# Six opening products in place of eleven, and weight blocks queued ahead of a table, in a Fourier attention kernel

## The chip, the core and the metric

The kernel runs on one core of a Trainium2 chip. The core has five engines, each with an instruction stream of its own that it works off in order: TensorE (PE in the profile, its weight loads are shown apart as PEld), VectorE (DVE), ScalarE (ACT), GpSimd (POOL) and SyncE (SP), which here issues all transfers. TensorE reads from the core's SBUF memory and writes to PSUM, from which DVE and ACT fetch the results. The metric is the device time of one execution in microseconds (us), the median of three runs.

## What is computed

The reference is a chain of three blocks over 4 batches of 1088 tokens with 128 features. In short:

```python
q_p, k_p = phi(q), phi(k)                      # outer product of two 8-wide projections: 64 features
kv, z = einsum('bhsf,bhsd->bhfd', k_p, v), sum(k_p)
attn  = (q_p @ kv) / (q_p @ z + 1e-6)          # linear attention, 4 heads of 32
x     = attn, heads side by side               # 4 x 1088 x 128
u     = x + real(fft over tokens and features of x)
x2    = u + relu(norm(u) @ w_ch1) @ w_ch2      # channel block
h     = relu(x2 @ w_in); uu, v = halves of h
out   = (uu * (w_spatial @ norm(v) + b)) @ w_out
```

The Fourier transform is computed as matrix products with tables of cosines and sines. [...]

## The kernel before

For each batch the kernel runs these stages. `keys` and `queries` build the features: for each of three chunks of tokens, TensorE projects (`abp`), ACT copies (`ab`), and DVE forms the outer products (`pp`); TensorE then sums keys against values (`kv`, copied to `kvz`), transposes the queries' features (`qps`, copied to `qp` by ACT), and multiplies the two (`nm`); DVE divides (`rd`, `ub`). `fourier_seq` folds the tokens with a product (`rp`) and additions on DVE (`eo`, `fe`, `l_`, `lrb`) and transforms along tokens with the table `tr` (and its rest `trr`) in 16 pairs of passes named `dft`; `fourier_feat` transforms along features with the table `dd` (`ups`, `urm`) and adds to `ub`. `channel` normalises (`un`), transposes (`t`), and runs the channel block (`h_`, `c`) and the first half of the last block (`v_ps`, `v`), ending in `vh` and `vlo`. `spatial` is the large product over tokens (`ac`), three passes for each piece, against the split weights `wsh` and `wsl`, which are made on the way from the loaded `wst`.

`from_f64` turns a block of raw 64-bit weights (`wraw`, 128 x 256 numbers) into 32-bit ones with five DVE instructions (lines 312, 315 to 318), three on ACT (311, 313, 314) and one on POOL (320); `weight` then splits the result into two parts (ACT line 333, POOL line 114). Ten such blocks exist; the buffers of `from_f64` are two deep.

`warm(n)` issues n products of a tile of zeros (`wp<-a`, line 519) that nothing uses. They stand in the program before everything else, after `rp` (10) and ahead of the channel block of batch 0 (20).

The program text writes batch 0's attention and transform, then its channel block, then `keys(1)` and `queries(1)`; a scheduler that weighs priorities and estimated times decides the order on each engine. Products marked with `tc.keep_in_program_order` keep their order among TensorE's. So an edit of the text can move many instructions. The transfers go through SP's queue in the order of the schedule, at most eight outstanding, since a transfer reuses the semaphore of the one eight places before it, and waits for that one's landing. `kt` and `qt` share ten buffers (`kq`), so a transfer for batch 2 also waits until TensorE has read the one whose buffer it takes.

Of the kernel before, what the change touches and what calls it, by code (L numbers as in the profile page):

```python
# [65 lines left out]
def fourier_attention_gmlp_kernel(  # L66
# [258 lines left out]
    def weight_load(tag, *blocks):  # L325
        t = const.tile([P, len(blocks), 512], I32, tag=tag, name="wraw")
        for i, (n, src, k) in enumerate(blocks):
            nc.sync.dma_start(out=t[:, i, :], in_=src.bitcast(I32)[:, 512 * k:512 * k + 512])
            wraw[n, k] = t[:, i, :]
# [8 lines left out]
    def loads(b):  # L338
        for tag, src in (("kt", kT), ("qt", qT)):
            for c in range(3):  # L340
                x = loaded[b, tag, c] = ca.tile([P, 384], F32, tag="kq", bufs=10, name=tag)
                nc.sync.dma_start(out=x, in_=src[b, :, 384 * c:384 * c + 384])
            if b == 0 and tag == "kt":
                nc.sync.dma_start(out=prm, in_=perm)
        for c in range(3):
            vx = loaded[b, "vx", c] = ca.tile([P, 3, 4, 33], F32, tag="vx", bufs=5, name="vx")
            nc.sync.dma_start(out=vx, in_=vt[b, :, 3 * c:3 * c + 3, :, :])
# [168 lines left out]
    def warm(n):  # L516
        wp = psy.tile([P, 512], F32, tag="us", bufs=1, name="wp")
        for i in range(n):
            tc.keep_in_program_order(mm(out=wp, lhsT=wz[:, 0:128], rhs=wz, start=True, stop=True))

    warm(11)
    raw0 = pre.tile([P, 128], I32, tag="un", bufs=2, name="raw")
    nc.sync.dma_start(out=raw0, in_=sblk.bitcast(I32))
    from_f64(raw0, 64, sb_s, True)
# [5 lines left out]
    blocks = [("w1", 0), ("w1", 1), ("w2", 0), ("w2", 1), ("wi", 2), ("wi", 3), ("wi", 0), ("wi", 1), ("wo", 0), ("wo", 1)]  # L530
    srcs = {"w1": w1, "w2": w2, "wi": win, "wo": wout}
    def load_raw(tag, part):
        weight_load(tag, *[(n, srcs[n], k) for n, k in part])

    loads(0)
    nc.sync.dma_start(out=tr, in_=trig)
    nc.sync.dma_start(out=trr, in_=trig_r)
    load_raw("wsl0", blocks[:6])
    nc.sync.dma_start(out=dd, in_=ddft)
    loads(1)  # L540
    load_raw("wsh0", blocks[6:])
# [209 lines left out]
```

## Time and profile before

| | |
|---|---|
| median of 3 runs | 462.87 us (462.74 to 463.55) |
| the profiled execution | 462.66 us, of which the span of the trace is 460.7 us |
| PE busy in the span | 441.3 us (96%) |
| DVE, ACT, POOL busy | 276.4, 191.7 and 68.4 us |
| mean granted clock of TensorE | 0.984 of full |

A busy share is the share of the span in which an engine works at an instruction. For TensorE it includes products that run at the lower of its two clocks (1.2 GHz in place of 2.4 GHz), and the products of zeros. Time is to be had where TensorE stands still, where it runs at the lower clock, or where it computes what nobody uses.

### The profile page before, as it was taken

The page shows a single profiled execution, that of the slowest core. Times are in us where ns is not written, and L with a number is a line of the kernel's source. Part 1 is how long each engine was busy: PE and PEld are TensorE (multiplying, and loading weights), DVE is VectorE, ACT ScalarE, POOL GpSimd, SP SyncE. Part 2 cuts the span into 40 slices and gives each one's busy share as a digit, 9 for nine tenths or more (in the row PEclk, how much of TensorE's full clock was granted, in tenths as well). Part 3 has the DMA queues.
Part 4 walks back from the last instruction along what each step waited for, and adds up shares of the span by engine and source line. Part 5 has one row for each costly group of instructions (what it writes and reads, how often), then busy time and mean ns, then how long its engine had stood idle before and what let it go on. Part 6 is the DMA issues. An engine that isn't in the chain of part 4 may idle for free.

```text
span 460.7 us, 7484 instructions
## 1 busy us (share of the span) xinstructions
PE 441.3 (96%) x2893; PEld 405.5 (88%) x2893; DVE 276.4 (60%) x685; ACT 191.7 (42%) x448; POOL 68.4 (15%) x105
## 2 busy tenths in 40 slices
PE   8889699899999999999999999999999999999996
PEld 7766589567879789899999999999999999999995
DVE  5688988987563596789736363883645456222221
ACT  3545596365223154456524243552423335212221
POOL 2154485572110150000000000000000000000000
PEclk9979799999999999999999999999999999999999
DMA  8992132011003100000000000000000000000000
GB/s 254 359 314 97 52 92 83 0 39 34 0 1 93 38 17 1 0 1 20 14 1 0 18 0 1 18 1 14 2 0 18 0 19 1 14 1 17 1 17 16
DMA packets 13007, 19.29 MB, mean 42 GB/s; under 512 B 1446, under 2 KB 11436, under 8 KB 12844
## 3 DMA queue, kind: packets, MB, share of 16 engines
q1 hardware_dynamic: 12972, 18.82, 12.7%
q8 instruction: 23, 0.38, 0.4%
q14 instruction: 12, 0.10, 0.1%
HBM read 16.58 MB, written 2.23 MB: 41 GB/s over the span
## 4 chain that ended last, share of the span: by engine, by line
PE 77%; issue 9%; DVE 9%; ACT 3%; POOL 1%; POOLq 0%; DVEq 0%; ACTq 0%
PE ac L605 12%; PE ac L604 12%; PE ac L606 12%; PE dft L462 3%; PE v_ps L254 2%; PE v_ps L256 2%; PE c L225 2%; PE c L227 2%; PE c L226 2%; PE v_ps L255 2%; PE nm L408 2%; PE ac L612 2%; PE ac L611 1%; PE u_ps L597 1%; PE u_ps L598 1%
## 5 line engine op out<-in xcount | busy, mean ns | idle before, releaser
L606 PE MATMUL ac<-wsh,vlo 128*128 128x384 f32 (+1 forms) x384 | 126.3, 329 | 2.2 <-POOL vlo L114 2.2
L604 PE MATMUL ac<-wsh,vh 128*128 128x384 f32 (+1 forms) x384 | 126.7, 330 | 0.1
L605 PE MATMUL ac<-wsl,vh 128*128 128x384 f32 (+1 forms) x384 | 126.4, 329 | 0.0
L606 PEld LDWEIGHTS ac<-wsh,vlo 128*128 128x128 f32 x384 | 72.0, 188 | 3.3 <-POOL vlo L114 3.1
L605 PEld LDWEIGHTS ac<-wsl,vh 128*128 128x128 f32 x384 | 72.1, 188 | 1.6 <-issue 0.8
L604 PEld LDWEIGHTS ac<-wsh,vh 128*128 128x128 f32 x384 | 72.1, 188 | 1.5 <-ACT vh L270 0.4
L615 DVE TENSOR_TENSOR uh<-ac,uh 128x384 f32<-128x384 f32 (+1 forms) x48 | 25.4, 529 | 57.0 <-PE ac L612 55.2
L601 ACT ACTIVATE uh<-u_ps 128x384 f32<-128x384 f32 (+1 forms) x48 | 22.6, 471 | 48.0 <-PE u_ps L599 45.5
L114 DVE TENSOR_TENSOR gl<-uh,gh 128x384 fp32r<-128x384 f32 (+1 forms) x48 | 26.2, 548 | 12.9 <-ACT gh L616 12.7
L245 POOL CAST xh<-xh 128x64 fp32r<-128x64 f32 x4 | 2.1, 514 | 201.8 <-ACT xh L242 201.8
L359 DVE TENSOR_TENSOR pp<-ab 128x768 f32<-128x768 f32 x23 | 23.7, 1062 | 11.8 <-ACT ab L355 11.4
L261 DVE BATCH_NORM_STATS2 bst<-vn 128x6 f32<-128x512 f32 x27 | 18.6, 693 | 16.7 <-ACT vn L259 16.6
L616 ACT CAST gh<-uh 128x384 fp32r<-128x384 f32 (+1 forms) x48 | 23.5, 492 | 12.2 <-DVE uh L615 11.9
L259 ACT ACTIVATE vn<-v_ps 128x512 f32<-128x512 f32 x27 | 16.0, 598 | 19.1 <-PE v_ps L256 18.6
L241 DVE TENSOR_TENSOR xt<-c,xt 128x384 f32<-128x384 f32 (+1 forms) x12 | 6.4, 534 | 27.7 <-PE c L227 27.7
L408 PE MATMUL nm<-kvz,qp 128*128 128x66 f32 x144 | 17.4, 271 | 0.0
L408 PEld LDWEIGHTS nm<-kvz,qp 128*128 128x128 f32 x144 | 17.2, 192 | 0.1
L282 ACT CAST vh<-vn 128x1024 fp32r<-128x1024 f32 x12 | 12.6, 1047 | 10.3 <-PE ac L605 8.2
L242 ACT CAST xh<-xt 128x384 fp32r<-128x384 f32 (+1 forms) x12 | 6.0, 497 | 26.0 <-DVE xt L241 26.0
L225 PE MATMUL c<-hh,w 128*128 128x384 f32 (+1 forms) x48 | 16.6, 346 | 0.0
L597 PE MATMUL u_ps<-sxh,wi 128*128 128x384 f32 (+1 forms) x48 | 16.3, 339 | 0.3 <-ACT uh L601 0.3
L227 PE MATMUL c<-hl,w 128*128 128x384 f32 (+1 forms) x48 | 16.3, 340 | 0.0
(714 smaller groups left out, 961.6 us busy)
## 6 DMA issues: line engine op xcount, KB each, us to landing
wst<-in_wsp SPq DMA_DIRECT2D x18, 192.0 KB, 2.8
vx<-in_vt SPq DMA_DIRECT2D x12, 198.0 KB, 4.3
kt<-in_kT SPq DMA_DIRECT2D x12, 192.0 KB, 6.2
qt<-in_qT SPq DMA_DIRECT2D x12, 192.0 KB, 4.4
w2st<-in_wsp SPq DMA_DIRECT2D x9, 160.0 KB, 4.1
tr<-in_trig SPq DMA_DIRECT2D x1, 1096.0 KB
wraw<-in_w SPq DMA_DIRECT2D x4, 256.0 KB, 7.7
wraw<-in_win SPq DMA_DIRECT2D x4, 256.0 KB, 5.2
```

The lines of the kernel that those rows point to most:

```text
L114: eng.tensor_tensor(out=lo, in0=x, in1=hi.bitcast(F32), op=ALU.subtract)
L225: mm(out=c2[:, 0:n], lhsT=wpart("w2", 0, 128 * m, 128), rhs=hh[:, 0:n], start=(m == 0), stop=False)
L227: mm(out=c2[:, 0:n], lhsT=wpart("w2", 0, 128 * m, 128), rhs=hl[:, 0:n], start=False, stop=(m == 3))
L359: (G if [b, tag[0], c] in [[3, 'k', 2]] else V).tensor_tensor(out=pp, in0=a_.unsqueeze(3).to_broadcast([P, 12, 8, 8]), in1=b_.unsqueeze(2) ...
L408: mm(out=nm[:, t, 2 * pr:2 * pr + 2, :].rearrange("p h d -> p (h d)"), lhsT=qp[:, pr, 128 * t:128 * t + 128], rhs=z[:, pr, :], start=True, ...
L597: mm(out=h_[:, 0:n], lhsT=wpart("wi", 0, 128 * m, 128), rhs=xh[:, 0:n], start=True, stop=False)
L601: A.activation(out=uh[:, 0:n], in_=h_[:, 0:n], func=ACTF.Relu)
L604: mm(out=ac[:, 0:n], lhsT=vh[:, k, ms], rhs=wsh[c][:, k, :], start=(k == 0), stop=False)
L605: mm(out=ac[:, 0:n], lhsT=vh[:, k, ms], rhs=wsl[c][:, k, :], start=False, stop=False)
L606: mm(out=ac[:, 0:n], lhsT=vl[:, k, ms], rhs=wsh[c][:, k, :], start=False, stop=False)
L615: V.tensor_tensor(out=uh[:, 0:n], in0=ac[:, 0:n], in1=uh[:, 0:n], op=ALU.mult)
L616: A.copy(out=gh[:, 0:n], in_=uh[:, 0:n])
```

## The change

Two lines differ. The opening products of zeros become six in place of eleven, and the transfers of six blocks of raw weights (`load_raw("wsl0", blocks[:6])`, each 256 KB: both blocks of `w1`, both of `w2`, two of `wi`) are written ahead of the transfers of the transform's table (`tr`, 1096 KB, and `trr`, 137 KB) in place of behind them.

```diff
-    warm(11)
+    warm(6)
     raw0 = pre.tile([P, 128], I32, tag="un", bufs=2, name="raw")
...
     loads(0)
+    load_raw("wsl0", blocks[:6])
     nc.sync.dma_start(out=tr, in_=trig)
     nc.sync.dma_start(out=trr, in_=trig_r)
-    load_raw("wsl0", blocks[:6])
     nc.sync.dma_start(out=dd, in_=ddft)
```

The scheduler answers with another order on every engine. On TensorE, from the ten products after `rp` of batch 0 (names as above; `abp<-sb_s,kt` and the first `kv` here belong to batch 1), the difference reads:

```order
 L519 MATMUL wp<-a_73 128x512 x10
-L353 MATMUL abp<-sb_s,kt 128x2x32 x9
-L353 MATMUL abp<-sb_s,qt 128x2x32 x3
-L376 MATMUL kv<-vx,pp 64x33 x36
-L397 MATMUL qps<-prm,pp 128x128
-L462 MATMUL dft<-tr,l__380 64x274
-L397 MATMUL qps<-prm,pp 128x128 x4
-L462 MATMUL dft<-tr,l__380 64x274 x3
...
+L462 MATMUL dft<-tr,l__375 64x274
+L353 MATMUL abp<-sb_s,kt 128x2x32 x2
+L462 MATMUL dft<-tr,l__375 64x274 x3
```

Batch 1's projections and key sums, which stood between the ten products and the transform, now stand behind it, but for two projections.

On DVE, in the order of before, this stands between the additions of batch 0 (`eo`, `lrb`) and the operands of the transform (`l_`):

```order
L438 TENSOR_TENSOR eo<-ub 128x512
L451 TENSOR_TENSOR lrb<-rs__378 32x63 x2
L312 TENSOR_SCALAR dy<-wraw 128x256
L315 TENSOR_SCALAR dx<-wraw 128x256
L312 TENSOR_SCALAR dy<-wraw 128x256
L315 TENSOR_SCALAR dx<-wraw 128x256
L359 TENSOR_TENSOR pp<-ab 128x768 x4
L447 TENSOR_TENSOR l__380<-fe 128x2x64 x2
```

In the changed kernel the same place on DVE reads:

```order
L316 TENSOR_SCALAR ds<-wraw 128x256
L438 TENSOR_TENSOR eo<-ub 128x512
L451 TENSOR_TENSOR lrb<-rs__373 32x63
L442 TENSOR_TENSOR fe<-eo 128x4x63
L451 TENSOR_TENSOR lrb<-rs__373 32x63
L447 TENSOR_TENSOR l__375<-fe 128x2x64 x2
L438 TENSOR_TENSOR eo<-ub 128x512
```

The four outer products of batch 1 are gone from here to behind the channel block's first instructions, and the first weight blocks' conversions have moved ahead: eight of their DVE instructions now stand between batch 0's sixth `pp` and its first `rd`. On ACT three of them now stand among the six copies of the queries' transposes:

```order
L385 COPY kvz_84<-kv 64x2x33
L311 ACTIVATE dr<-wraw 128x256
L402 COPY qp<-qps 128x384 x2
L313 ACTIVATE dy<-dy,cst 128x256
L402 COPY qp<-qps 128x384 x2
L314 ACTIVATE dy<-dy,cst 128x256
L402 COPY qp<-qps 128x384 x2
```

Before, the six copies followed `kvz` without a break, and the conversions came behind them.

## Rows read from the trace of the kernel before

**Rows 1.** The page, part 2: TensorE's granted clock, in tenths, in 40 slices of the span.

```profile
PEclk9979799999999999999999999999999999999999
```

**Rows 2.** By stage: us; busy PE, PEld, DVE, ACT, POOL; granted clock, DMA share, GB/s.

```profile
0.00:4.00 4.00, 2.43 (x6) 1.95 (x7) 1.86 (x11) 2.41 (x5) 3.14 (x13) 1.00 0.42 120
...
5.80:12.40 6.60, 6.60 (x110) 6.43 (x109) 4.75 (x6) 1.92 (x6) 0.00 (x0) 1.00 1.01 350
...
50.15:57.00 6.85, 6.11 (x20) 5.05 (x21) 6.07 (x17) 3.37 (x9) 2.63 (x4) 0.50 0.02 8
57.00:79.20 22.20, 21.95 (x141) 19.59 (x140) 19.17 (x44) 18.90 (x45) 16.61 (x15) 1.00 0.33 91
79.20:106.50 27.30, 24.00 (x162) 18.03 (x160) 25.55 (x50) 14.05 (x32) 17.48 (x22) 1.00 0.08 22
106.50:460.70 354.20, 347.84 (x2217) 329.18 (x2213) 188.56 (x467) 130.41 (x299) 13.09 (x29) 1.00 0.04 12
```

**Rows 3.** Timeline, 0 to 14 us: start, us, engine, line, operation, out<-in [idle before].

```profile
1.57 4.74 PE L519 MATMUL wp<-a 128*128 128x512 f32 x11 [1.57 <-DVE a L514]
...
3.90 0.22 DVE L320 TENSOR_TENSOR sb_s<-dr,ds 128x64 f32<-128x64 f32 x1
...
6.15 2.12 PE L353 MATMUL abp<-sb_s,kt 128*128 128x64 f32 x18
...
7.45 2.20 SPq L328 DMA_DIRECT2D wraw<-in_w  x4
...
10.21 2.29 PE L376 MATMUL kv<-vx,pp 128*64 128x33 f32 x72
...
11.21 1.83 DVE L359 TENSOR_TENSOR pp<-ab 128x768 f32<-128x768 f32 x2 [0.34 <-PE kv L376]
```

**Rows 4.** Timeline, 12 to 21 us: the queries of batch 0.

```profile
12.43 0.87 PE L397 MATMUL qps<-prm,pp 128*128 128x128 f32 x6
...
14.17 2.10 ACT L402 COPY qp<-qps 128x384 f32<-128x384 f32 x4 [0.25 <-PE qps L397]
...
15.59 3.46 PE L408 MATMUL nm<-kvz,qp 128*128 128x66 f32 x30
...
20.62 0.46 PE L429 MATMUL rp<-ub,prm 128*128 128x128 f32 x2 [1.56 <-DVE ub L418]
```

**Rows 5.** Timeline, 20 to 51 us: from the ten products to the channel block.

```profile
20.83 2.56 PE L519 MATMUL wp<-a 128*128 128x512 f32 x10
...
27.05 3.56 DVE L359 TENSOR_TENSOR pp<-ab 128x768 f32<-128x768 f32 x4
...
28.06 3.23 PE L376 MATMUL kv<-vx,pp 128*64 128x33 f32 x72 [2.05 <-DVE pp L359]
...
31.63 1.18 PE L462 MATMUL dft<-tr,l__380 128*64 128x274 f32 x2
...
38.41 0.62 PE L462 MATMUL dft<-trr,lrb 128*64 128x274 f32 x2
...
41.60 4.84 PE L519 MATMUL wp<-a 128*128 128x512 f32 x20
...
50.15 0.42 PE L199 MATMUL t<-prm,un 128*128 128x128 f32 x1 [3.31 <-DVE un L195]
```

**Rows 6.** Timeline: one step of the transform (a pair of passes) and the next.

```profile
37.02 0.39 PE L462 MATMUL dft<-tr,lz 128*64 128x274 f32 x1
...
37.25 0.39 PE L462 MATMUL dft<-tr,lz 128*64 128x274 f32 x1
```

**Rows 7.** Groups by line and shape, 0 to 60 us: count, busy us, mean ns, idle before.

```profile
L313 ACT ACTIVATE dy<-dy,cst 128x256 int32<-128x256 int32 x10 | 4.9, 504 | 4.3 <-DVE dy L312 4.3
...
L315 DVE TENSOR_SCALAR dx<-wraw 128x256 int32<-128x256 int32 x10 | 2.8, 276 | 0.0
```

**Rows 8.** Spatial weights: first use (timeline), and issue to landing (page, part 6).

```profile
58.41 0.92 ACT L134 CAST wsh<-wst 128x384 fp32r<-128x384 f32 x2
...
wst<-in_wsp SPq DMA_DIRECT2D x18, 192.0 KB, 2.8
```

## The prediction

> **What bounds the kernel now.** I read the profile from the whole to the place. The stages first [rows 2]: from 106.5 us to the end TensorE is busy for 347.8 of 354.2 us, so whatever the change does must reach the end through the time at which this saturated part begins. From 57 to 106.5 us two engines are near full: TensorE 45.95 of 49.5 us, DVE 44.7 of 49.5 us. The opening of 57 us is another thing. There TensorE waits and twice runs at the lower clock [rows 1]; from 50.15 to 57 us the granted clock is 0.50 [rows 2].
>
> The timeline shows who makes it wait. Eleven products of zeros take 0.43 us each (4.74/11), where ten of the same form take 0.256 us later [rows 3, 5]: 0.43 us for 512 columns is the 1.2 GHz level, although the view of stages prints 1.00 there. They are TensorE's first work, and the projections behind them begin at 6.15 us. Then the chain runs through DVE: `rp` waits 1.56 us for `ub` [rows 4], `kv` of batch 1 waits 2.05 us for `pp`, and the transform, from 31.63 to 39.03 us, begins only after DVE's four `pp` of batch 1 (3.56 us) and TensorE's `kv` of batch 1 (3.23 us), which stand ahead of it in the order though it needs neither [rows 5]. The channel block's first transpose comes at 50.15 us after a wait of 3.31 us for DVE [rows 5].
>
> **The change, step by step.** I follow the chain to that first transpose, and then subtract the work that is only put off.
>
> *Five products fewer.* Six end at 1.57 + 6 x 0.43 = 4.15 us. The projections need `sb_s`, ready at 4.12 us [rows 3], and the first `kt`: in the first 4 us 120 GB/s bring 480 KB [rows 2], which covers the 64 KB ahead of it and two chunks of 192 KB. So they begin at about 4.2 in place of 6.15 us. But the six chunks then wait for transfers: the first `qt` has landed by 7.45 us, where SP goes on to `wraw` behind it [rows 3], and at 350 GB/s [rows 2] the other two follow by 0.55 us each, 8.55 us. A chunk of six passes takes 0.7 us (2.12/18 x 6, [rows 3]), so the projections end at 9.3 us, the first sums of `kv` follow at once in place of at 10.21 us, and DVE's last two `pp`, which wait for `kv`, end at 12.1 in place of 13.04 us. Gain 0.9 us of the 2.15 us taken away.
>
> *Raw weights first.* The transfers ahead of both candidates come to 2.0 MB; the six blocks are 1.54 MB, the table 1.23 MB. At 350 GB/s from 7.45 us on, with some 1.0 MB still to land there, the first two blocks land by about 11.7 and the table by 18 us, where it would have landed by 14. The transform cannot ask for it before 24 us (below), so this delay costs nothing; without that cover it would cost the 4 us itself.
>
> *Conversions moved forward.* DVE waited 13.04 to 16.41 us; eight conversion instructions now stand there, 2.2 us at 0.276 us [rows 7], so they fit. On ACT three of them stand among the six `qp` copies: 1.5 us at 0.504 us [rows 7]. The copies ended at 16.27 us [rows 4]; now they end at 16.27 - 0.9 + 1.5 - 0.25 (ACT's own wait there) = 16.6 us. `rp` came 4.35 us behind them, through `nm` and `ub`, and I add 0.4 us for two more conversion instructions between `rd` and `ub` on DVE. So `rp` comes at 21.4 in place of 20.62 us: the gain of the opening is given back, and 0.8 us more.
>
> *The transform moved forward.* From the end of `rp` (21.08 us) to the transform's start (31.63 us) went 10.55 us, 3.56 of them for four `pp` [rows 5] and about 2.7 for ten conversion instructions at 0.276 us [rows 7]. Left are 4.3 us for the operands. I add 0.5 us for POOL's small copies, which now stand behind two conversions of its own. From 21.85 us this gives 26.6 us for the second pass of the transform (the first comes earlier). At full clock a step takes 0.23 us [rows 6], 16 steps 3.7 us, so it ends at 30.3 in place of 39.03 us. From its end to the first transpose went 50.15 - 39.03 = 11.1 us; the chain in it (`ups`, `ub`, statistics on DVE with eleven conversion instructions in place of twelve) is the same, and the twenty products beside it are hidden under DVE. First transpose: 41.4 us, **8.7 us earlier**.
>
> *What is put off.* DVE still has to do four `pp`, 3.56 us, and three conversion instructions, 0.9 us: 4.5 us that were done before 50.15 us. TensorE has three projections (six passes, 0.7 us), 36 products of `kv` (72 passes, 2.3 us by [rows 3]) and six transposes (0.9 us by [rows 4]): 3.9 us. They fall into the stage in which both are over 90% busy [rows 2], so I count them in full: the net gain is 8.7 - 4.5 = 4.2 us by DVE and 4.8 by TensorE. I take the smaller. The five products do not enter again, for the chain has passed them already.
>
> *The queue.* SP's transfers of the spatial weights now stand behind a `qt` of batch 2, whose buffer is free when TensorE has done batch 1's third projection, behind the twenty products: about 38 us (26.6 + 3.7 + 2.6 for `ups` and `urm` + 4.84 [rows 5]). They land 2.8 us after issue; eight of them by about 44 us. ACT's first use came 8.3 us after the first transpose [rows 5, 8], so at 49.7 us now: 5 us of cover, nothing to pay. If the twenty products ran at 0.43 us, 3.8 us of it would go, still nothing.
>
> *The clock.* In the channel block's first 6.85 us the clock was low, after TensorE had stood still for 3.31 us [rows 2, 5]. By the times above it stands still for about 1 us there. If the clock then stays up, some 14 products of 384 columns cost 0.17 in place of 0.32 us: up to 2.0 us more. I do not count it, and keep it for the range.
>
> The profiled execution took 462.66 us; 462.66 - 4.2 = 458.5. The median shown is 0.2 us above it, so 458.7; I put **458.6 us**.
>
> **The rivals.**
>
> *The transform still meets the lower clock.* Before, TensorE stood still for 2.05 us ahead of `kv`, and the clock was low soon after; the transform took 7.4 us [rows 5]. Now there is a wait of about 2 us ahead of `rp` and one of 1.3 us ahead of the transform's second pass. For it: the waits are alike. Against it: the ten products between. Then the transform ends at 34.0 us, and the net gain is 0.5 us: 462.3 us.
>
> *DVE takes it all back.* Four `pp` of 0.89 us fall between DVE's operations on the channel block's path; TensorE waits for each if nothing stands in. Four such waits beyond the counted work, 3.6 us, leave 0.6 us: 462.2 us. For it: DVE's 25.55 of 27.3 us from 79.2 us on [rows 2]. Against it: TensorE was busy for 21.95 of 22.2 us in the stage before, with two such `pp` in it.
>
> *Six products do not raise the clock (slower).* The eleven products and the passes behind them had the clock up by 6 us [rows 3]: the projections' passes of 0.118 us are those of the full level. If the clock stays low until the ten products, projections come to 1.4 us a chunk, their end to 12.6 in place of 9.3 us, and the 6.6 us of `qps` and `nm` [rows 4] to at most twice that: `rp` 9.9 us later. Gain 4.2 less 9.9: 468 us. It decides from a delay of 5 us of `rp` on. Against it: projections follow the six without a pause.
> The Trainium skill ("TensorE: Matmul & The Clock Gate", section "What's actually happening") says that the lower clock is the default and only TensorE's own activity lifts it. By that rule taking opening products away speaks against the change, and this rival is its price. The trace agrees as to the start, at 0.43 us a product, and no run yet shows a shorter opening.
>
> That the edit changes nothing is excluded: the orders differ on all engines.
>
> **How the numbers follow.** Forecast 0.64; lower clock in the transform 0.14; DVE takes it back 0.08; slow opening, or a wait I have not seen, 0.14. The two middle cases lie close to no change: two thirds of their 0.22 fall within 0.2% (0.9 us, about what a measurement of this kernel can tell from no change), the rest is split, mostly to faster. Faster 0.69, same 0.16, slower 0.15. The forecast's own range is 456.3 (with the clock's 2.0 us) to 460.8 us (half of the gain); to leave out no more than 2 in 10 the range reaches up over the two middle cases: 456.2 to 463.4 us.
>
> **What would show it.** The first projection at 4.2 us; the sixth `pp` done by 12.1; `rp` at 21.4, no earlier than before; the transform from 26.6 to 30.3 us with steps of 0.23 us; no wait of TensorE for the table; the first transpose at 41.4 us; TensorE saturated some 4 us sooner. The forecast is wrong if the clock is low at 27 to 31 us, if passes of the projections take over 0.2 us after 7 us, or if TensorE's idle time between the first transpose and saturation grows by more than 3 us.

## The result and the profile after

The changed kernel took 465.58 us (median of four executions, 464.32 to 466.55) against 462.81 us (462.58 to 463.55) for the kernel before on the same chip: a ratio of 1.0056 [1.0029, 1.0082]. It became slower by 0.6%, where 458.6 us had been forecast. The profiled execution took 466.55 us, its span is 464.8 us. Ratios here and below are to the kernel before on the same chip. Where the executions of a kernel below fall on two levels, the times of both are given, since the two levels are the finding; ratios leave out executions more than 1.5% above the fastest of their kernel.

The timeline of the changed kernel, rows of TensorE and one each of DVE, POOL and ACT, from the start to the channel block's first transpose (called T1 from here on, the 50.15 us row of [rows 5]) and just behind it:

```profile
1.57 2.93 PE L519 MATMUL wp<-a 128*128 128x512 f32 x6 [1.57 <-DVE a L514]
4.65 4.10 PE L353 MATMUL abp<-sb_s,kt 128*128 128x64 f32 x18 [0.16 <-DVE sb_s L320]
...
8.55 4.05 PE L353 MATMUL abp<-sb_s,qt 128*128 128x64 f32 x18
...
10.42 0.96 DVE L359 TENSOR_TENSOR pp<-ab 128x768 f32<-128x768 f32 x1 [0.32 <-ACT ab L355]
...
12.52 2.78 PE L376 MATMUL kv<-vx,pp 128*64 128x33 f32 x48
...
17.07 1.33 PE L397 MATMUL qps<-prm,pp 128*128 128x128 f32 x5
...
22.80 3.37 PE L408 MATMUL nm<-kvz,qp 128*128 128x66 f32 x28
27.86 0.46 PE L429 MATMUL rp<-ub,prm 128*128 128x128 f32 x2 [1.69 <-DVE ub L418]
28.08 2.55 PE L519 MATMUL wp<-a 128*128 128x512 f32 x10
...
36.39 0.62 PE L462 MATMUL dft<-trr,lrb 128*64 128x274 f32 x2
...
48.83 0.33 PE L199 MATMUL t<-prm,un 128*128 128x128 f32 x1 [1.26 <-DVE un L195]
...
50.99 0.73 POOL L114 TENSOR_TENSOR wo<-dr,wo 128x256 fp32r<-128x256 f32 x1 [0.52 <-ACT wo L333]
51.75 0.44 ACT L311 ACTIVATE dr<-wraw 128x256 f32<-128x256 uint32 x1 [0.84 <-DMA wst<-in_wsp]
```

Read the second row against the same row of before [rows 3]. Eighteen passes of the projections took 4.10 us, 0.228 us each, where they took 2.12 us, 0.118 us each. Nothing interrupts them: the next row begins at 8.55 us, without a wait. So this is TensorE at the lower of its two clocks. It stays there through `kv` (2.78 us for 48 products, 1.59 us for 48 in the kernels below that have the clock up) and until the last `nm`, 28 of which take 3.37 us, 0.12 us each, which is the full level. DVE's outer products now come 1.28 us apart and wait 0.32 us for ACT, as in the row at 10.42 us; ACT waits for TensorE. `rp` came at 27.86 us, where 21.4 had been forecast and 20.62 measured before [rows 4]. From there on the program runs much as forecast, only later (the second pass of the transform came 5.3 us behind `rp`, forecast 5.2), and T1 comes at 48.83 us.

The page's row of the granted clock does not show this:

```profile
PEclk9999899999999999999999999999999999999999
```

A slice is 11.6 us. The first two print the full level, although the passes in them took twice their time: as in the opening of before, what lies ahead of the first recorded change of the clock (here the rise near 23 us) is printed as full. The durations decide.

The span splits at T1. These are the stages of before and then of the changed kernel, columns as in [rows 2]:

```profile
50.15:460.70 410.55, 399.91 (x2532) 371.84 (x2532) 239.35 (x574) 166.72 (x383) 49.81 (x70) 0.99 0.06 17
```

```profile
0.00:48.83 48.83, 41.56 (x272) 34.92 (x272) 32.95 (x105) 22.28 (x58) 15.56 (x35) 1.00 0.62 209
48.83:464.80 415.97, 403.42 (x2616) 375.21 (x2616) 244.14 (x581) 169.67 (x391) 50.63 (x70) 0.99 0.07 22
```

T1 came 1.3 us earlier than before, in place of 8.7, and what follows T1 became 5.4 us longer.

### The profile page after: what moved, and what is told of

It reads as the page before. It is cut to its first block, busy times and chain, and to the rows that moved or that the text cites. A ratio compares the mean times of both kernels' runs of the same rounds, so it can differ in the third digit from the quotient of the medians.

```text
span 464.8 us, 7480 instructions
## 1 busy us (share of the span) xinstructions
PE 445.0 (96%) x2888; PEld 410.1 (88%) x2888; DVE 277.1 (60%) x685; ACT 192.0 (41%) x448; POOL 66.2 (14%) x105
## 4 chain that ended last, share of the span: by engine, by line
PE 69%; DVE 11%; issue 10%; ACT 3%; DMA 3%; POOL 3%; SPq 1%; POOLq 0%; DVEq 0%; ACTq 0%
PE ac L605 12%; PE ac L606 12%; PE ac L604 12%; PE dft L462 2%; PE v_ps L256 2%; PE c L227 2%; PE v_ps L254 2%; PE ac L612 1%; PE ac L611 1%; PE u_ps L597 1%; PE u_ps L598 1%; PE u_ps L599 1%; DMA dd<-in_ddft 1%; PE v_ps L255 1%; PE c L225 1%
## 5 line engine op out<-in xcount | busy, mean ns | idle before, releaser
L114 DVE TENSOR_TENSOR gl<-uh,gh 128x384 fp32r<-128x384 f32 (+1 forms) x48 | 25.9, 541 | 13.4 <-ACT gh L616 13.3
L259 ACT ACTIVATE vn<-v_ps 128x512 f32<-128x512 f32 x27 | 16.1, 598 | 19.2 <-PE v_ps L256 18.7
L256 PE MATMUL v_ps<-wi,xl 128*128 128x512 f32 x36 | 15.3, 424 | 1.2 <-DVE xl L114 1.2
```

Of the source, the lines that this page charges most:

```text
L114: eng.tensor_tensor(out=lo, in0=x, in1=hi.bitcast(F32), op=ALU.subtract)
L256: mm(out=h_, lhsT=xl[:, cs], rhs=wt["wi"][:, 2:4, 0, :], start=False, stop=True)
```

## The experiments

The theory after the result: six opening products do not bring the clock up, so all work up to `rp` runs at half speed; the earlier weights and the earlier transform do gain. Rivals: the transfers in their new order or the new order of the instructions cost the time. Below, "weights first" is the order of transfers of the changed kernel, "table first" that of the kernel before.

**Eight opening products, all else as changed.** The order on each engine is that of the changed kernel, row for row.

```diff
-    warm(6)
+    warm(8)
```

> Eight opening products, raw weights first: the order on PE, DVE and ACT is that of the changed kernel row for row, only the count of products differs. Clock theory (the six products did not lift TensorE's clock, and the projections after them do not lift it either): if eight lift it, projections run at 0.118 us a pass by 7 us, the first transpose comes at 42 to 43 us in place of 48.8, and the time falls by 5 to 6 us to 459.5 to 461. If eight are still too few, all stays as in the changed kernel, 465 to 466. Rearrangement theory (the new order itself costs the time, by work put off into the full stage): 464 us or more, whatever the clock does.

Measured: 460.13 us (459.56 to 460.88, six executions), ratio 0.9949 [0.9934, 0.9964]. The timeline of TensorE, and the stages:

```profile
1.57 3.78 PE L519 MATMUL wp<-a 128*128 128x512 f32 x8 [1.57 <-DVE a L514]
5.15 2.94 PE L353 MATMUL abp<-sb_s,kt 128*128 128x64 f32 x18
7.93 2.17 PE L353 MATMUL abp<-sb_s,qt 128*128 128x64 f32 x18
...
21.35 0.77 PE L429 MATMUL rp<-ub,prm 128*128 128x128 f32 x2 [1.69 <-DVE ub L418]
21.77 4.61 PE L519 MATMUL wp<-a 128*128 128x512 f32 x10
...
42.46 0.33 PE L199 MATMUL t<-prm,un 128*128 128x128 f32 x1 [1.30 <-DVE un L195]
```

```profile
21.77:26.40 4.63, 4.63 (x13) 3.21 (x13) 3.76 (x12) 0.92 (x3) 2.27 (x8) 0.50 0.85 249
...
31.90:42.46 10.56, 9.26 (x58) 7.53 (x57) 10.29 (x42) 7.08 (x20) 5.32 (x7) 1.00 0.20 59
...
42.46:459.00 416.54, 404.15 (x2616) 375.83 (x2616) 244.29 (x581) 169.62 (x391) 50.61 (x70) 0.99 0.07 22
```

Two products more, and the second 18 passes run at 0.12 us each; `rp` comes 6.5 us earlier than in the changed kernel, T1 6.4 us. The rest after T1 is the same within 0.6 us. The clock of the opening is the whole of the loss, and neither the order of the transfers nor that of the instructions is: both are unchanged here.

**Six opening products alone,** the table first as before.

```diff
-    warm(11)
+    warm(6)
```

> Six opening products, table first as before: only the first part of the change; the order is nearly that of before (26 differing lines on TensorE). Clock theory: the clock stays low until 20 us or later, the queries' products end 6 to 7 us later than before, and the kernel takes 467 to 470 us, more than the changed kernel, because it has the loss without the gain of the new order. Rearrangement theory: 460.5 to 463 us, as before or a little faster, since the order that costs the time is not there.

Measured: 467.54 us, ratio 1.0077 [1.0044, 1.0109]; but nine executions took 466.1 to 468.1 us and three 461.6 to 462.1. The profiled one took 467.33 us:

```profile
4.30 2.67 PE L353 MATMUL abp<-sb_s,kt 128*128 128x64 f32 x18
7.89 3.49 PE L353 MATMUL abp<-sb_s,qt 128*128 128x64 f32 x18 [0.92 <-DMA qt<-in_qT]
...
18.77 0.34 PE L408 MATMUL nm<-kvz,qp 128*128 128x66 f32 x2
...
24.92 0.46 PE L429 MATMUL rp<-ub,prm 128*128 128x128 f32 x2 [1.56 <-DVE ub L418]
```

```profile
8.60:18.70 10.10, 10.10 (x100) 9.30 (x100) 2.88 (x3) 2.82 (x8) 0.00 (x0) 0.50 1.03 389
```

This edit by itself is a loss, but in this execution not because the clock never came up. The keys' 18 passes took 2.67 us, between the 2.1 us of the full and the 4.1 us of the lower level; the projections then waited 0.92 us for `qt`, and from 8.6 to 18.7 us the granted clock is 0.50. The clock came up among the keys' passes and fell again. So six products lost the clock in two ways: low from the start in the profile of the changed kernel, up and lost again here. That the wait for `qt` made it fall is not shown.

**Weights first alone,** with eleven products.

```diff
     loads(0)
+    load_raw("wsl0", blocks[:6])
     nc.sync.dma_start(out=tr, in_=trig)
     nc.sync.dma_start(out=trr, in_=trig_r)
-    load_raw("wsl0", blocks[:6])
```

> Eleven opening products, raw weights first: only the second part of the change; the transform again stands ahead of batch 1's outer products. Clock theory: the clock is up by 6 us as before, the first transpose comes at 42 to 44 us, 459 to 461.5 us. Rearrangement theory: 464 us or more.

Measured: 460.28 us (459.95 to 461.02), ratio 0.995 [0.9934, 0.9965]; `rp` at 21.78 us, the transform's second pass at 26.99, T1 at 42.65. This edit by itself is a gain of 2.3 us (0.5% by the ratio); the forecast's 4.2 less the 0.9 that it gave to the shorter opening would be 3.3.

**Seven opening products,** and **the changed kernel once more.**

```diff
-    warm(6)
+    warm(7)
```

> Seven opening products, raw weights first, again the changed kernel's order row for row. Both theories: tells only where the count begins to matter. Clock theory: either a low clock to 20 us and 465 to 466.5 us, or a clock that is up by 7 us and 459.5 to 461 us, nothing in between in one execution; a spread over both among its runs if it depends on when the kernel starts. Rearrangement theory: 464 us or more.

> The changed kernel once more, for a count of its executions. Clock theory, with chance in it (whether six products lift the clock depends on where they fall when the kernel starts, as seven and the first part alone showed two times each): most executions at 464 to 467 us, and some, up to one in three, at 459.5 to 460.5 us, the time of eight products. Rearrangement theory, which the runs with eight and eleven already speak against: one time only, 464 to 467 us.

Measured with seven: 460.43, 459.82, 459.97, 459.95, and twice 469.7 us. With six again: 464.31, 465.31, 466.39, 469.34, 469.51 and 470.03 us, ratio 1.0113 [1.0075, 1.0151]. The profiled execution with six took 469.34 us:

```profile
22.38 6.08 PE L408 MATMUL nm<-kvz,qp 128*128 128x66 f32 x28
30.15 0.77 PE L429 MATMUL rp<-ub,prm 128*128 128x128 f32 x2 [1.69 <-DVE ub L418]
30.57 4.40 PE L519 MATMUL wp<-a 128*128 128x512 f32 x10
...
51.02 0.33 PE L199 MATMUL t<-prm,un 128*128 128x128 f32 x1 [1.31 <-DVE un L195]
```

Here the 28 `nm` also ran at the lower level, 0.217 us each, and the clock came up only in the ten products behind `rp`, near their end. That spreads the changed kernel's times: `rp` at 27.86 us gave 466.55, at 30.15 us 469.34. In none of its ten executions did it come near 460 us. Two of the ten were profiled; in the two at 464.3 us the mean granted clock is 0.978, against 0.995 and 0.993 in the profiled ones, so more of the lower clock lies behind the first recorded change there. Where, is not shown.

**Six more products in TensorE's wait ahead of `rp`,** eight at the opening; and the same with four in place of ten behind `rp`.

```diff
+        if b == 0:
+            warm(6)
         rp = ...
...
-            warm(10)
+            warm(4)
```

> Eight opening products, raw weights first, and six further products put ahead of batch 0's fold product, where TensorE waits 1.7 us for DVE; the ten behind the fold stay. If that wait is what lets the clock fall (low from 20.5 to 27.4 us with eight products, so that the ten took 4.6 us in place of 2.6 and the transform's second pass came at 28.0): the ten take 2.6 us, the second pass comes at 26.6 us, set by DVE, the first transpose 1 to 1.4 us earlier, and the time is 458.7 to 459.3 us. If the clock falls anyway, or DVE sets the end: 460 to 460.5 us. Slower, 461 us, if the six take 0.43 us each and delay the fold.

> As the run with six products in the wait, but only four behind the fold in place of ten. If the ten only fill DVE's time: the transform begins when DVE has its operands, the same time as with ten within 0.3 us or a little less. If they hold the clock for the transform: its steps take 0.45 us, the transform ends 2 to 3.5 us later, 460.5 to 462 us.

Measured: 460.54 us with ten kept (nine executions at 459.4 to 461.0, three at 466.0 to 470.3), ratio 0.9981 [0.9952, 1.001]; 459.19, 459.99, 460.43 and 470.44 us with four. The timeline and the stages of the first:

```profile
19.42 1.64 PE L521 MATMUL wp<-a 128*128 128x512 f32 x6
21.31 0.46 PE L431 MATMUL rp<-ub,prm 128*128 128x128 f32 x2 [0.25 <-DVE ub L418]
21.52 2.54 PE L521 MATMUL wp<-a 128*128 128x512 f32 x10
...
42.31 0.33 PE L199 MATMUL t<-prm,un 128*128 128x128 f32 x1 [1.30 <-DVE un L195]
```

```profile
30.47:42.31 11.84, 9.49 (x57) 7.51 (x57) 11.31 (x44) 7.38 (x20) 6.35 (x9) 1.00 0.21 61
```

The clock now holds through the transform, which ends 1.4 us earlier (30.47 against 31.9 us), and T1 moves by 0.15 us. Between the two DVE is busy for 11.31 of 11.84 us, in the kernel with eight for 10.29 of 10.56 us: DVE sets T1, and the transform's speed is worth next to nothing. The kernel with four agrees: its granted clock is 0.50 from 25.9 to 29.2 us, the transform ends at 31.55 us, and T1 still comes at 42.42 us. **Eleven opening products with six in the wait** say the same:

> Eleven opening products as before, the raw weights ahead of the table, and six further products of zeros ahead of rp of batch 0, where TensorE waits 1.6 to 1.9 us for DVE; the ten behind rp kept. Theory (the clock falls because TensorE stands still ahead of rp; products there hold it, but DVE's conversions set the first transpose of the channel block): the clock stays up through the transform, which ends near 30.8 us, the first transpose comes at 42.3 to 42.7 us all the same, and the time is 460.0 to 460.7 us in every execution, as with eleven opening products alone. Rival (the lower clock behind rp costs the end something): 459.0 to 459.7 us.

Measured: 460.88 us (459.87 to 461.94), ratio 0.9959 [0.9943, 0.9974], T1 at 43.29 us, 0.6 us later than I had expected, since `rp` came only at 22.42 us.

**The transform early without the weights early.** With 14 opening products and the table first, the scheduler puts the transform ahead of batch 1's outer products, as the change does.

```diff
-    warm(11)
+    warm(14)
```

> Fourteen opening products, table first: with this count the scheduler puts the transform ahead of batch 1's outer products, as with raw weights first. It asks whether the gain of 2.3 us needs the transfers' place. If the gain is the transform's place in the order: the opening loses 1.0 to 1.3 us to three more products, and the time is 461 to 462 us. If it is the weights' earlier landing and conversion: 463 to 464 us.

Measured: 464.99 us (464.34 to 465.7), ratio 1.0057 [1.0042, 1.0073], more than either of my expectations. The transform ends at 33.75 us, 5.3 us earlier than before, but T1 comes at 46.91 us after a wait of 3.56 us for DVE, and the rest after T1 is 416.9 us long. Less is won at T1 (3.2 us) than is put off (6.3 us). DVE's first conversion starts at 18.25 us here, behind the first `rd`; with weights first DVE converts ahead of it, where it would wait. That the blocks have to be on the chip early for this is how I read it; it is not shown alone, since the three further products cost time here too (`rp` at 22.49 us).

**Eight products more behind batch 0's last `kv`,** six at the opening, weights first.

```diff
     keys(0)
+    warm(8)
     queries(0)
```

> The changed kernel, with eight further products of zeros written between the keys and the queries of batch 0, so that they stand between the last sums of kv and the queries' transposes. Before them the same narrow passes as in the changed kernel. Theory (the narrow passes of the projections and sums do not lift the clock, wide products do): the opening stays at the lower level, projections at 0.23 us a pass, and the clock first rises within or just behind the eight products, near 17 to 21 us, in every execution; rp near 29 to 30 us, time 464 to 468 us with a spread under 2 us. Rival (when the clock rises has nothing to do with which passes run, it varies by itself): the first rise stays near 23 us or near 35 us from execution to execution, and the times spread over 464 to 472 us.

> The kernel with six opening and eight late products once more, to see a profile of one of the executions near 464 us. Theory (wide products lift the clock, narrow passes don't): in such an execution the projections take 0.23 us a pass, and the clock first rises within or just behind the eight products, at 16 to 21 us, in place of 23 or 35 us as in the changed kernel; rp near 28 us. Rival (the rise has nothing to do with which passes run): first rise behind 22 us.

Measured: 457.92, 458.41, 458.99 and seven at 463.5 to 465.9 us; again, 457.74, 457.82, 457.97, 458.56, then 462.42, 463.97 twice and 464.57 us. Both profiles are of executions near 458 us:

```profile
1.57 2.93 PE L519 MATMUL wp<-a 128*128 128x512 f32 x6 [1.57 <-DVE a L514]
4.29 2.94 PE L353 MATMUL abp<-sb_s,kt 128*128 128x64 f32 x18
7.07 2.17 PE L353 MATMUL abp<-sb_s,qt 128*128 128x64 f32 x18
...
42.47 0.28 PE L199 MATMUL t<-prm,un 128*128 128x128 f32 x1
```

```profile
42.47:455.96 413.49, 400.71 (x2594) 373.23 (x2593) 242.03 (x578) 168.91 (x390) 50.73 (x70) 1.00 0.07 21
```

So with six products the clock can be up by 7 us and stay up through the sums: the second 18 passes run at 0.12 us each. My expectation, that the opening would stay low in every execution, was wrong. To see the others, **the same with five at the opening:**

> The kernel with eight late products of zeros, opened by five products in place of six, to see those eight behind an opening that stayed at the lower clock. Theory (wide products lift the clock, narrow passes don't): no execution near 458 us; projections at 0.23 us a pass; the clock first rises within or just behind the eight products at 16 to 21 us; 463 to 466 us throughout. Rival (the rise has nothing to do with which passes run): the first rise comes behind 22 us, or still early in some executions.

Measured: 464.92 us (463.55 to 465.11, seven executions), ratio 1.0045 [1.0031, 1.006].

```profile
4.40 4.07 PE L353 MATMUL abp<-sb_s,kt 128*128 128x64 f32 x18 [0.33 <-DMA kt<-in_kT]
...
12.24 2.78 PE L376 MATMUL kv<-vx,pp 128*64 128x33 f32 x48
...
16.78 3.42 PE L519 MATMUL wp<-a 128*128 128x512 f32 x8
20.03 0.71 PE L397 MATMUL qps<-prm,pp 128*128 128x128 f32 x5
...
28.08 0.46 PE L429 MATMUL rp<-ub,prm 128*128 128x128 f32 x2 [1.69 <-DVE ub L418]
...
48.53 0.28 PE L199 MATMUL t<-prm,un 128*128 128x128 f32 x1
```

```profile
48.53:462.00 413.47, 400.70 (x2594) 373.13 (x2593) 242.06 (x578) 169.00 (x390) 50.65 (x70) 1.00 0.07 21
```

The passes ahead of the eight late products are slow, five `qps` behind them take 0.71 us where they took 1.33 us in the changed kernel, and the eight are 3.25 us from the next row, where eight of 0.43 us are 3.4: the clock came up towards the end of the eight. And the rest after T1 is 413.47 us against 413.49 us with the early rise. T1 lies 6.06 us later and the span is 6.0 us longer: the clock of the opening goes into T1, and T1 into the end, one to one.

**Eleven, and eight, at the opening of that kernel:**

> The kernel with eight late products of zeros, opened by eleven products in place of six; behind the first sums of kv its order on TensorE is that of the kernel with eight late products. Theory (with the clock up from the opening this order is worth what three of ten executions of that kernel showed, 457.9 to 459.0 us, and six opening products only made it a matter of chance): all executions between 457.5 and 459.5 us, ratio to the kernel before 0.990 to 0.993; the first transpose of the channel block at 42.5 to 43.5 us and 413 to 414 us behind it. Rival (the short opening itself is part of the gain, since everything starts sooner): 460 to 461 us, as the other kernels with eleven opening products.

> The same kernel opened by eight products. Theory (with the clock up early, each opening product costs its time at the end, since the whole chain starts later: 458.1 us at six, 460.9 us at eleven): 458.8 to 459.6 us in the executions with an early rise, which are four of five or more; the others near 465 us. Rival (the order of the kernel with eleven, not the opening's length, cost the 2.8 us): 457.9 to 458.5 us.

Measured with eleven: 460.89 us (459.89 to 462.32), ratio 0.9959 [0.9943, 0.9975], T1 at 44.33 us. With eight: five executions at 459.4 to 459.9 us, four at 460.9 to 463.0, three at 467.7 to 468.0; T1 at 44.16 us. My expectation of 458 us in every execution with eleven fell: the 458 us need the short opening too. Two products more cost 1.4 to 1.7 us at T1, more than their 0.86 us; in both profiles `rp` waits 2.1 us in place of 1.69 for DVE. Whether that comes from the later start or from DVE's order, which differs in places, I did not separate.

None of these beats the plain versions in every execution. The one to use is weights first with the eleven products kept, 460.28 us.

## Why the prediction was wrong

*Five products fewer.* This is the step that failed. It priced the projections behind six products at 0.118 us a pass, and the rival of a low clock was set aside with "projections follow the six without a pause". They did follow almost at once (a pause of 0.16 us in the first profile, none in the second) and ran at 0.228 and 0.224 us. `rp` came at 27.86 in place of 21.4 us. The row of [rows 3] had shown the passes at full clock only behind eleven products; it held nothing on six. The rival that I gave 0.14, slower at 468 us from a delay of `rp` of 5 us on, came true: the delay was 6.5 us in the first profile and 8.75 us in the second, the times 466.55 and 469.34 us. Its sum took the clock to be low until the ten products in every execution; in the second profile that is what happened, in the first it came up within `nm`, hence the shorter time. Low from the start is not the only form: with the table first the clock came up and was lost again.

*Raw weights first, conversions moved forward.* Right. No product waited for the table; its landing is 8.3 us after issue by the page, issue at 9.27 us, so 17.6 (forecast 18). With the clock up `rp` came at 21.35 us (eight products) and 21.31 us (eight, and six more in the wait), forecast 21.4. The forecast was for six, whose projections were to begin at 4.2 us and not at 5.15 us, so that it fits this well is in part luck.

*The transform moved forward.* Right where the clock was held: second pass at 26.59 us (forecast 26.6), end at 30.47 (30.3). The rival of a lower clock there was in part right as an event: with eight products the granted clock is 0.50 behind `rp`, the ten products take 4.61 us, and the transform ends 1.4 us later than where the clock was held. Its price, 3.7 us, was wrong: T1 came 0.15 us later, since DVE sets T1. For the same reason the 11.1 us from the transform's end to T1 are no constant (10.6 and 11.8 us here), and T1 came at 42.3 to 42.7 us in place of 41.4: 7.7 us earlier than before with eight products, not 8.7.

*What is put off.* Mis-sized. With eight products the rest after T1 is 416.54 against 410.55 us, 6.0 us longer, where 4.5 had been counted. DVE has 4.9 us more there (244.29 against 239.35), as counted within 0.4; TensorE has 4.2 us more (404.15 against 399.91) and stands still for 12.4 in place of 10.6 us. I had taken the larger of the two engines' shares and no further waits; the waits were the 1.8 us. So the gain with the clock up is 7.7 - 6.0 = 1.7 us between the two profiles and 2.4 us (0.51%) by the ratio, not 4.2.

*The clock in the channel block,* kept for the range with 2.0 us. In the changed kernel TensorE waited 1.26 us ahead of T1, with eight products 1.30 us, and in both the clock fell again soon after. These are the stretches at 0.50 with eight products, and with eight and six more in the wait ahead of `rp`:

```profile
44.42:47.83 3.41, 3.39 (x10) 2.67 (x11) 2.97 (x10) 1.54 (x4) 0.73 (x1) 0.50 0.71 249
```

```profile
43.40:50.10 6.70, 5.97 (x18) 5.34 (x19) 6.26 (x18) 3.59 (x9) 2.18 (x4) 0.50 0.49 169
```

The second is twice as long, and the rest after T1 is 416.54 and 416.58 us, in the same order of instructions from T1 on. In the changed kernel's two profiles it is 415.97 and 416.58 us, with 0.50 from 50.4 to 53.7 us and from 51.7 to 58.4 us. So 3.4 us more at the lower clock went with 0.6 us at most, where the 2.0 us kept for 6.85 us would have made 1.0 us. With eight late products TensorE does not wait there at all, as the T1 rows show, and the rest is 413.5 us. That is 3 us less than 416.5; DVE has 2.3 us less of put-off work in it. The clock's part is not told apart from the order's there; the pairs above speak for the order.

*The queue.* Right as to the cost, by what the profiles show. The transfers that stand behind `qt` were issued from 40.23 us on with eight products (forecast 38), and ACT's first copy of `wst` came at 50.33 us there, without a wait (forecast 49.7); in the changed kernel it came at 56.63 us, without a wait too. The profile puts ACT's wait of 0.84 us at 51.75 us down to `wst`, but the instruction that waited reads `wraw`, and it started 0.03 us after POOL had finished with the block before (50.99 + 0.73 us, in the first timeline). With eight products the same pair stands at 45.38 us. So I read it as a wait for POOL.

## What to carry to other kernels

A count of warming products can be a margin against chance, as it was here, and not only a cost to trim: measure it over many executions, since here kernels with six to eight had fast executions and slow ones. Read TensorE's clock in an opening from the distance of equal products, not from a clock row that has no record yet. Where two edits come together, price each against the stage it changes: here one gained 0.5%, the other lost more than that (0.8% with the table first), and a profile of the pair alone would have condemned both.

## What was unexpected of the hardware

Whether the clock was up in the opening varied from execution to execution of the same program. With the times near a kernel's lowest taken as a clock that was up early and stayed up (only some of these executions were profiled): six products, 3 of 12, 0 of 10 and 7 of 18 executions (table first, changed, eight late); seven, 4 of 6; eight, 18 of 22 in the first three kernels that have eight, and in the fourth all but three of 12 lie apart from its slow level; with eleven and fourteen no execution lay apart. The Trainium skill ("TensorE: Matmul & The Clock Gate", section "What's actually happening") says that the number of slow products at a kernel's start varies from run to run; these counts agree with it in that, and the low stretch reached to 22.8 us and beyond 28 us here.

What TensorE did before each rise was not what I had in mind. From 4.65 us on in the first profile of the changed kernel, and from 4.3 us on in the second, it worked almost without pause at the projections, sums, transposes and `nm`, and the clock stayed at the lower level until 22.8 us in the one and beyond 28 us in the other. With eight products of 512 columns among the same passes the clock was up before these eight ended. Once it was up, as in the kernel before, the same passes ran to the end at the full level; only in the profile with the table first it fell among them, behind the wait of 0.92 us for `qt`. The theory of my expectations, that wide products lift the clock and narrow passes do not, is not shown by this: in the first profile of the changed kernel it came up within `nm`, over 18 us after the last wide product. And the same wait of 1.69 us ahead of `rp` was followed by ten products at the lower level (4.61 us) with eight opening products, and at the full one (2.55 us) in the changed kernel; what decides that stays open.
